# Softmax of two head pairs at once on neighbouring PSUM banks, in a fused attention and MLP kernel

## The chip, the cores and the metric

The kernel runs on one core of one Trainium2 chip. A core has a matrix engine (PE in the profile, with its weight loads shown apart as PEld), a vector engine (DVE), a scalar engine (ACT), a general engine (POOL) and queues that start DMA transfers (SP). Each engine runs its own instructions in the order in which the program holds them, and an instruction that waits for a semaphore holds up all that stand behind it on its engine. The metric is the device time of one execution in microseconds; less is better.

## What is computed

Chunked attention with a short left and right context and eight memory keys, then an MLP with a leaky activation on its output:

```python
B, H, S, D = 4, 8, 768, 64          # batches, heads, tokens, head size
for c in range(S // 32):            # chunks of 32 queries
    keys   = mem_k[8] + k[16 left .. 32 .. 8 right]     # values likewise
    scores = q_c @ keys.T / sqrt(D)
    a      = exp(scores - max(scores));  a /= sum(a) + 1e-9
    out[c] = a @ values
x = out as (3072 tokens, 512)
h = x @ w_in                        # 512 -> 2048
g = max(h, 0) + alpha * min(h, 0)   # alpha per hidden column
y = g @ w_out                       # 2048 -> 512
```

All data are fp32. An fp32 product of the MLP is made of three fp32r products: each operand is split into a high and a low part, and low*high, high*low and high*high are summed in one PSUM bank.

## The kernel before

**Tiling.** The 3072 tokens lie in 8 blocks of 384 (`BT`). A block's attention is cut into four units, one for each pair of heads; unit `u` belongs to block `u // 4`. The MLP of a block is cut into 16 slices `f` of 128 hidden columns.

**Units 0 to 7** (`NWIN`), the attention of blocks 0 and 1, come in the prologue and do the softmax on whole windows (`windows(u)`): scores on PE into a bank of the pool `ps_s` (L271), the maximum on DVE (L439 or L441, then L443), the subtraction (L447), exp on ACT (L451), the sum and its inverse (L455, L458), the scaling on POOL (L468, L472), transposes on PE (`turn`, L480), copies on ACT (L485), the product with the values (L493), and the split of the result into high (ACT, L408) and low (DVE, L412). Score products alternate between two tiles, with tags `s0` and `s1`, each one PSUM bank. `stir` (L257) writes products of a constant tile `busy` that nobody reads: `STIR = (8, 2, 1)` puts 8 of them ahead of the scores of unit 0, 2 ahead of the scores of each other one of the eight units, and 1 ahead of each of the eight turns.

**Units 8 to 31** use other code (L289 to L375), and run between the slices of the blocks ahead of them.

**A slice** `f` of a block has these steps (`hidden`): `up`, 12 products of 128x384 into one bank of `ps_h` (L614, three for each of four parts `k` of x); `below` on ACT, which reads that bank (L623); `bend` on DVE, which reads it too (L626); the high part (ACT or DVE, L632) and low part (DVE, L636) of g; and `down`, 9 products of 128x512 into three banks that collect the block's output (L644). The hidden banks alternate by `place`, the number of the slice in the whole program: tag `h0` for even places, `h1` for odd ones. `ORDER` lets blocks 0 and 1 alternate for their first 9 slices (places 0 to 17); then come the other slices of block 0 and of block 1, and then one block after the other, so that later blocks begin at places 32, 48, 64, 80, 96 and 112.

**Weights** come packed from memory. While block 0 runs, each slice's w_in and w_out are decoded (`decode`, L556 to L583): a gather of half-words (L564, on DVE or on ACT), shifts and joins on DVE, and conversions on ACT and DVE.

**The order of the program.** Each step names the engine, a cost and the keys that it reads and writes (`step` ends in `Plan.add`). `Plan.send` then runs a list scheduler over all steps: it takes an engine's ready step with the longest chain behind it, by the costs and due times, and writes its instructions. So an engine's order is the plan's, and a changed cost or key moves steps far away. The waits, on the other hand, do not come from those keys: they are put in as the instructions are written, by the tiles that they touch. The pools have one buffer for each tag; two tags of a pool are two tiles.

`zero` (L517, L520) clears three buffers of the later units on POOL in the prologue.

Of the kernel before, what the change touches and what calls it, by code (L numbers as in the profile page):

```python
# [9 lines left out]
F32 = mybir.dt.float32  # L10
# [8 lines left out]
P = 128  # L19
# [62 lines left out]

STIR = (8, 2, 1)

DUE_WEIGHTS, DUE_VALUES = 3, 4


NWIN, NSET = 2 * NPAIR, 4

STARTS_WIN = (0, 2 * LEFT, NKT - KW)  # L90
# [66 lines left out]
def body(ctx: ExitStack, tc: tile.TileContext, qvw, kw, first, w_in, w_out, alpha, out):  # L157
# [34 lines left out]

    es = [at.tile([P, NJ * 2, KW + 1], F32, name="e", tag=f"e{i}") for i in range(2)]
    for e in es:
        nc.gpsimd.memset(e[:, :, KW:], 1e-9)
    for ew in ews:
# [61 lines left out]

    def score_products(u):
        blk, pr = divmod(u, NPAIR)  # L260
# [3 lines left out]
        st["s"] = s_ps[:, :2 * NJ * KW].rearrange("p (n k) -> p n k", k=KW)  # L264
        t = early[u % NSET]
        q = t[:, :NQ].rearrange("p (c x) -> p c x", c=NT * NJ)
        keys = t[:, NQ:NQ + NT * NKT].rearrange("p (t k) -> p t k", t=NT)
        for n in range(2 * NJ):
            for i in range(2):
                t, j = n // NJ * 2 + i, n % NJ  # L270
                nc.tensor.matmul(  # L271
                    out=st["s"][i * 2 * CH:(i + 1) * 2 * CH, n],
                    lhsT=q[:, t * NJ + j],
                    rhs=keys[:, t, STARTS_WIN[j]:STARTS_WIN[j] + KW],
                    start=True, stop=True,
                )

    def head_products(u):

        st = state[u]  # L280
        st["s"] = [ps_s.tile([P, 512], F32, name="s_ps", tag=f"s{h2}")[:, :NJ * KW].rearrange("p (n k) -> p n k", n=NJ)
                   for h2 in range(2)]
# [20 lines left out]
    def scores(u):  # L303
# [11 lines left out]
        def exps(i):  # L315
            if i == 0:
                st["e"] = at.tile([P, NJ * 2, KW], F32, name="e", tag=f"e{u % 2}")
                st["den"] = sm.tile([P, NJ * 2, 1], F32, name="den", tag=f"den{u % 3}")
# [7 lines left out]
        for i in range(NJ * 2):  # L326
            step(ACT, 0.54, partial(exps, i), reads=[("s", i % 2), ("mx", u % 3)],
                 writes=[("e", u % 2, i), ("den", u % 3, i)] if i else e_keys(u) + den_keys(u), rest=due(u))

# [89 lines left out]
    def load_first(u):  # L419
# [8 lines left out]
        step(SP, 0.78, partial(load, NQ + NT * NKT, NQ + NT * NKT + NV), writes=[("fv", u % NSET)], rest=due(u))  # L428

    def windows(u):  # L430

        st = state[u]
        sk, tks, ak = ("s", u % 2), [("o", 0), ("o", 1)], ("o", 2) if u % 2 else "a"
        ek = [("ew", u % NPT)]

        def top():
            s = st["s"]
            if u // NPAIR % 2 == 0:
                nc.vector.memset(s[0:2 * CH, 0, 0:LEFT], NEG)  # L439
            else:  # L440
                nc.vector.memset(s[2 * CH:4 * CH, 2 * NJ - 1, KW - NM - RIGHT:KW - NM], NEG)  # L441
            st["mx"] = sm.tile([P, NJ * 2, 1], F32, name="mx", tag=f"mx{u % 3}")
            nc.vector.tensor_reduce(out=st["mx"], in_=s, axis=AX.X, op=ALU.max)  # L443

        def less():
            st["e"] = es[u % 2][:, :, :KW]
            nc.vector.tensor_tensor(out=st["e"], in0=st["s"], in1=st["mx"].broadcast_to([P, NJ * 2, KW]),  # L447
                                    op=ALU.subtract)

        def exps():  # L450
            nc.scalar.activation(out=st["e"], in_=st["e"], func=AF.Exp, scale=SCALE)  # L451

        def total():
            st["den"] = sm.tile([P, NJ * 2, 1], F32, name="den", tag=f"den{u % 3}")
            nc.vector.tensor_reduce(out=st["den"], in_=es[u % 2], axis=AX.X, op=ALU.add)  # L455

        def inverse():
            nc.vector.reciprocal(out=st["den"], in_=st["den"])  # L458

# [39 lines left out]

        step(PE, 1.2, partial(score_products, u), reads=[("qk", u % NSET)], writes=[sk], rest=due(u))  # L500
        step(DVE, 0.66, top, writes=[sk, ("mx", u % 3)])
        step(DVE, 0.55, less, reads=[sk, ("mx", u % 3)], writes=e_keys(u))
        step(ACT, 0.52, exps, writes=e_keys(u))
        step(DVE, 0.56, total, reads=e_keys(u), writes=den_keys(u))
        step(DVE, 0.19, inverse, writes=den_keys(u))
        step(POOL, 0.62, partial(scale, 0), reads=den_keys(u) + e_keys(u), writes=ek)
        step(POOL, 0.5, partial(scale, 1), reads=den_keys(u) + e_keys(u), writes=ek)
        step(PE, 0.90, turn, reads=ek + ["eye"], writes=tks, rest=due(u, 1))
        for t in range(2):
# [37 lines left out]
    def decode_part(k, parts):  # L547
# [53 lines left out]
    def hidden(blk, f, first_f, last_f):  # L601
# [36 lines left out]
        def down(o_ps):  # L638
            if f == first_f:
                banks = [(ps_o, f"o{i}") for i in range(NTT)] if not joint else [(ps_s, "s0"), (ps_s, "s1"), (ps_a, "a")]  # L640
                o_ps.extend(pool.tile([P, DM], F32, name="o_ps", tag=tag) for pool, tag in banks)
            for tt in range(NTT):
# [63 lines left out]
    def unit_begins(u):  # L706
        if u < NWIN:
            windows(u)
        else:
            scores(u)  # L710
# [113 lines left out]
```

## Time and profile before

| | |
|---|---|
| median of three runs | 613.23 us (612.78 to 613.33) |
| the profiled execution, whole | 612.68 us |
| its span, first to last instruction | 610.9 us |
| granted TensorE clock, mean | 1.000 |
| POOL busy | 34.6 us |
| DMA: read and written | 41.95 MB and 6.29 MB |

The span is 1.8 us shorter than the time of the same execution; what lies outside it is start and end. A row of a timeline below reads: start, duration, engine, line and operation, output and inputs with their shapes, the count, and in brackets the idle time ahead of it on its engine and what ended that.

### The profile page before, as it was taken

What the parts mean: (1) busy time and instruction counts of PE and PEld (TensorE: products, weight loads), DVE (VectorE), ACT (ScalarE), POOL (GpSimd) and SP (SyncE); (2) the same over time, 40 slices, a digit from 0 to 9 for tenths busy, and PEclk for the clock granted to TensorE, in tenths of its full rate; (3) what the DMA queues carried; (4) which work ended last, traced back from release to release, by engine and by line L of the source; (5) the groups of instructions that cost most, each with busy time, mean ns of one, the idle gap of its engine ahead of it and who ended that gap; (6) DMA issues with size and microseconds to landing.
All of it is one profiled execution on the core that took longest, in us unless ns stands there. A gap on an engine that the chain in (4) does not pass through costs nothing.

```text
span 610.9 us, 11593 instructions
## 1 busy us (share of the span) xinstructions
PE 605.0 (99%) x4622; PEld 532.9 (87%) x4622; DVE 404.5 (66%) x1012; ACT 215.6 (35%) x596; POOL 34.6 (6%) x61
## 2 busy tenths in 40 slices
PE   8999999999999999999999999999999999999997
PEld 5789999889898888989889889888889888989986
DVE  5888999886777656666666666666666656633332
ACT  3788787634223222322223122322123222121111
POOL 3500000000000000000000000000000000000000
PEclk9999999999999999999999999999999999999999
DMA  8999400114121111201113101221002100010001
GB/s 340 352 408 410 164 0 1 33 32 150 25 96 49 50 50 49 99 3 50 49 50 101 42 9 49 84 67 50 20 30 101 50 18 19 0 54 1 0 1 52
DMA packets 20934, 48.99 MB, mean 80 GB/s; under 512 B 2448, under 2 KB 5520, under 8 KB 20880
## 3 DMA queue, kind: packets, MB, share of 16 engines
q1 hardware_dynamic: 20880, 48.25, 22.3%
q8 instruction: 36, 0.59, 0.4%
q14 instruction: 18, 0.15, 0.1%
HBM read 41.95 MB, written 6.29 MB: 79 GB/s over the span
## 4 chain that ended last, share of the span: by engine, by line
PE 97%; DVE 1%; DMA 1%; issue 0%; ACT 0%; SPq 0%; ACTq 0%
PE h_ps L614 44%; PE o_ps L644 44%; PE a_ps L375 3%; PE s_ps L289 3%; PE s_ps L257 1%; PE s_ps L271 1%; DMA w_t<-w_in 1%; PE a_ps L493 1%; PE o_ps L480 0%; DVE w_t L568 0%; PE o_ps L257 0%; DVE mx L443 0%; DVE e L447 0%; DVE w_t L564 0%; DVE xl L412 0%
## 5 line engine op out<-in xcount | busy, mean ns | idle before, releaser
L614 PE MATMUL h_ps<-xh,w 128*128 128x384 f32 x1024 | 261.6, 336 | 0.0
L644 PE MATMUL o_ps<-w,gh 128*128 128x512 f32 x768 | 240.7, 395 | 0.0
L614 PEld LDWEIGHTS h_ps<-xh,w 128*128 128x128 f32 x1024 | 185.7, 188 | 4.2
L614 PE MATMUL h_ps<-xl,w 128*128 128x384 f32 x512 | 174.6, 341 | 0.1
L644 PEld LDWEIGHTS o_ps<-w,gh 128*128 128x128 f32 x768 | 144.0, 188 | 27.8
L644 PE MATMUL o_ps<-w,gl 128*128 128x512 f32 x384 | 150.1, 391 | 0.0
L623 ACT ACTIVATE g<-h_ps 128x384 f32<-128x384 f32 x128 | 63.4, 496 | 245.2 <-PE h_ps L614 236.0
L626 DVE SCALAR_TENSOR_TENSOR g<-g,rise,h_ps 128x384 f32<-128x384 f32 x128 | 78.3, 612 | 94.4 <-ACT g L623 93.3
L361 DVE STREAM_TRANSPOSE pt<-e 32x192 f32<-32x192 f32 (+1 forms) x336 | 99.3, 300 | 11.1 <-POOL e L340 5.9
L614 PEld LDWEIGHTS h_ps<-xl,w 128*128 128x128 f32 x512 | 96.2, 188 | 6.5 <-DVE xl L412 0.3
L644 PEld LDWEIGHTS o_ps<-w,gl 128*128 128x128 f32 x384 | 72.1, 188 | 12.5
L636 DVE TENSOR_TENSOR gl<-g,gh 128x384 fp32r<-128x384 f32 x128 | 71.1, 557 | 4.6 <-ACT gh L632 1.4
L632 DVE CAST gh<-g 128x384 fp32r<-128x384 f32 x104 | 37.2, 360 | 54.2 <-PE o_ps L644 52.4
L320 ACT ACTIVATE e<-s_ps,mx 128x64 f32<-128x64 f32 x144 | 43.3, 320 | 39.7 <-DVE mx L313 39.7
L340 POOL TENSOR_TENSOR e<-e,den 128x384 f32<-128x384 f32 x24 | 20.1, 839 | 467.1 <-DVE den L337 457.4
L408 ACT CAST xh<-a_ps 128x384 fp32r<-128x384 f32 x32 | 15.4, 480 | 55.4 <-PE a_ps L375 53.6
L320 ACT ACTIVATION_READ_ACCUMULATOR e<-s_ps,mx 128x1 f32 x144 | 30.5, 212 | 0.0
L375 PEld LDWEIGHTS a_ps<-pt,v_t 128*64 128x64 f32 x384 | 16.6, 136 | 8.5 <-issue 8.5
L375 PE MATMUL a_ps<-pt,v_t 128*64 128x96 f32 x384 | 21.1, 252 | 0.0
L583 DVE TENSOR_TENSOR w<-a,w 128x1024 fp32r<-128x1024 f32 (+1 forms) x18 | 20.3, 1135 | 0.0
L572 DVE SCALAR_TENSOR_TENSOR a<-a,w_t 128x1024 int32<-128x1024 int32 (+1 forms) x18 | 19.8, 1102 | 0.2
L556 ACT ACTIVATE a<-w_t 128x1024 f32<-128x1024 f32 (+1 forms) x18 | 18.8, 1048 | 2.9 <-DMA w_t<-w_in 1.6
(52 smaller groups left out, 278.3 us busy)
## 6 DMA issues: line engine op xcount, KB each, us to landing
w_t<-w_in SPq DMA_DIRECT2D x16, 512.0 KB, 10.2
w_t<-w_out SPq DMA_DIRECT2D x16, 512.0 KB, 10.2
qk<-kw SPq DMA_DIRECT2D x24, 272.0 KB, 3.7
v_t<-qvw SPq DMA_DIRECT2D x24, 256.0 KB, 2.8
out<-o_t SPq DMA_DIRECT2D x24, 256.0 KB, 2.1
early<-first SPq DMA_DIRECT2D x8, 656.0 KB, 5.9
qk<-qvw SPq DMA_DIRECT2D x24, 192.0 KB, 3.6
early<-first SPq DMA_DIRECT2D x8, 256.0 KB, 5.9
```

Of the source, the lines that this page charges most:

```text
L320: nc.scalar.activation(out=st["e"][:, i], in_=st["s"][h2][:, n], func=AF.Exp, scale=SCALE, bias=st["mx"][:, n, h2:h2 + 1], accum_out=st["d ...
L340: nc.gpsimd.tensor_tensor(out=st["e"], in0=st["e"], in1=st["den"].broadcast_to([P, NJ * 2, KW]), op=ALU.mult)
L361: nc.vector.transpose(out=pts[u % NPT][quad * CH:(quad + 1) * CH, j, t0:t0 + n1 - n0].rearrange("p t h q -> p (t h) q"), in_=(st["e"], zer ...
L375: nc.tensor.matmul(out=st["a"][h2 * D:(h2 + 1) * D, t * TQ:(t + 1) * TQ], lhsT=st["v"][:, t, h2, :], rhs=pts[u % NPT][:, :, t, h2, :], sta ...
L572: nc.vector.scalar_tensor_tensor(out=d["a"], in0=d["a"], scalar=3, in1=d["t"][:, :, :, 1], op0=ALU.logical_shift_left, op1=ALU.bitwise_or)
L583: nc.vector.tensor_tensor(out=d["w"][:, :, 1], in0=d["a"].bitcast(F32), in1=d["w"][:, :, 0].bitcast(F32), op=ALU.subtract)
L614: nc.tensor.matmul(out=h["ps"][:, :BT], lhsT=ws[f, 0][:, wk, k * P:(k + 1) * P], rhs=xs[first + k][xk], start=(k == 0 and n == 0), stop=(k ...
L623: nc.scalar.activation(out=h["g"], in_=h["ps"][:, :BT], func=AF.Relu, scale=-1.0)
L626: nc.vector.scalar_tensor_tensor(out=h["g"], in0=h["g"], scalar=rise[:, f:f + 1], in1=h["ps"][:, :BT], op0=ALU.mult, op1=ALU.add)
L632: copy(out=h["gh"], in_=h["g"])
L636: nc.vector.tensor_tensor(out=h["gl"], in0=h["g"], in1=h["gh"].bitcast(F32), op=ALU.subtract)
L644: nc.tensor.matmul(out=o_ps[tt], lhsT=h[gk][:, tt * P:(tt + 1) * P], rhs=ws[f, 1][:, wk], start=(f == first_f and i == 0), stop=(f == last ...
```

## The change

- `STIR` becomes `(8, 0, 0)`: 2 unread products go ahead of each of scores 1 to 7, 1 ahead of each of eight turns, 22 in all.
- The two tiles of the pool `ps_s` become one tile `s_banks` of two banks, and the two of `ps_h` one tile `h_banks` of two banks. Everything that used a tile now uses a half: scores and hidden products, and the joint output of block 1's first 9 slices.
- A new function `softmax(us)` does maximum, subtraction, exp, sum and inverse for one or two units with one instruction each. `GROUPS` leaves units 0 and 1 alone and joins 2 with 3, 4 with 5 and 6 with 7. Units 4 and 5 put their scores into `h_banks`, the others into `s_banks`. The exp tiles become two rings of two units.
- `zero` moves from the prologue to the place where block 0's slice 9 is decoded, behind the decoding of slice 8.
- The gather of the half w_out of slice 0 goes from ACT to DVE.
- The plan's costs of a unit's scores and of a turn fall from 1.2 to 0.76 and from 0.90 to 0.68.

```diff
-STIR = (8, 2, 1)
+STIR = (8, 0, 0)
+GROUPS = ((0,), (1,), (2, 3), (4, 5), (6, 7))
...
+    h_banks = ps_h.tile([P, 2, 512], F32, name="h_ps")
+    s_banks = ps_s.tile([P, 2, 512], F32, name="s_ps")
...
-    es = [at.tile([P, NJ * 2, KW + 1], F32, name="e", tag=f"e{i}") for i in range(2)]
+    es = [at.tile([P, 2, NJ * 2, KW + 1], F32, name="e", tag=f"ee{i}") for i in range(2)]
...
-    def score_products(u):
+    def score_products(u, bank):
-        s_ps = ps_s.tile([P, 512], F32, name="s_ps", tag=f"s{u % 2}")
-        stir(s_ps, STIR[0] if u == 0 else STIR[1])
+        stir(bank, STIR[0] if u == 0 else STIR[1])
...
+    def softmax(us):
+        u0, n = us[0], len(us)
+        two, keys = (h_banks, ["h0", "h1"]) if u0 == 4 and n == 2 else (s_banks, [("s", 0), ("s", 1)])
+        here, ring = slice(u0 % 2, u0 % 2 + n), u0 // 2 % 2
+        keys, e = keys[here], es[ring][:, here]
...
+        view = two[:, here, :2 * NJ * KW].rearrange("p b (n k) -> p b n k", k=KW)
+        def top():
...
+            nc.vector.tensor_reduce(out=d["mx"], in_=view, axis=AX.X, op=ALU.max)
+        def less():
+            nc.vector.tensor_tensor(out=e[..., :KW], in0=view, in1=d["mx"].broadcast_to([P, n, NJ * 2, KW]),
+                                    op=ALU.subtract)
...
+        for u, key in zip(us, keys):
+            step(PE, 0.76, partial(score_products, u, two[:, u % 2]), reads=[("qk", u % NSET)], writes=[key], rest=due(u))
+        step(DVE, 0.13 + 0.04 + 0.4 * n + 0.065 * n, top, writes=keys + mk)
+        step(DVE, 0.14 + 0.4 * n, less, reads=keys + mk, writes=ek)
...
-            step(*((ACT, 1.37) if k[1] else (DVE, 0.72)), partial(gather, [nc.scalar.copy if k[1] else nc.vector.tensor_copy]),
-                 writes=r)
+            copy = nc.scalar.copy if k == (1, 1) else nc.vector.tensor_copy
+            step(*((ACT, 1.37) if k == (1, 1) else (DVE, 0.72)), partial(gather, [copy]), writes=r)
...
-                h["ps"] = ps_h.tile([P, 512], F32, name="h_ps", tag=hk)
+                h["ps"] = h_banks[:, place % 2]
...
-            banks = [(ps_o, f"o{i}") for i in range(NTT)] if not joint else [(ps_s, "s0"), (ps_s, "s1"), (ps_a, "a")]
+                if joint:
+                    o_ps.extend([s_banks[:, 0], s_banks[:, 1], ps_a.tile([P, DM], F32, name="o_ps", tag="a")])
...
-    step(POOL, 3.0, zero, writes=["e2"] + [("pt", i, j) for i in range(NPT) for j in range(len(TURNS))] + [("ew", i) for i in range(NPT)])
...
+        if (blk, f) == (0, NJOINT):
+            step(POOL, 3.0, zero, reads=[("w", 1, f - 1, 1)], writes=["e2"] + [("ew", i) for i in range(NPT)]
+                 + [("pt", i, j) for i in range(NPT) for j in range(len(TURNS))])
```

In the prologue, PE's rows begin with the unread products and go on as follows before the change. `early` are the transferred queries and keys of a unit, `ew` the scaled softmax, a name that begins with DMAHW is a transfer's semaphore, and the others are named by their engine; a row with `x11` stands for eleven more alike.

```order
L271 MATMUL s_ps<-early 64x64 [waits DMAHW0_49]
L271 MATMUL s_ps<-early 64x64 x11
L257 LDWEIGHTS busy
L257 MATMUL s_ps<-busy 128x512
L257 LDWEIGHTS busy
L257 MATMUL s_ps<-busy 128x512
L271 MATMUL s_ps<-early 64x64 [waits DMAHW1_49]
L271 MATMUL s_ps<-early 64x64 x11
L257 LDWEIGHTS busy [waits DVE_49]
L257 MATMUL s_ps<-busy 128x512 [waits PE_49]
```

The same place of PE after the change, from the scores of unit 0 to the first turn:

```order
L274 MATMUL s_ps<-early 64x64 [waits DMAHW0_49]
L274 MATMUL s_ps<-early 64x64 x11
L274 MATMUL s_ps<-early 64x64 [waits DMAHW1_49,DVE_49]
L274 MATMUL s_ps<-early 64x64 x11
L274 MATMUL s_ps<-early 64x64 [waits DMAHW2_49,DVE_49]
L274 MATMUL s_ps<-early 64x64 x11
L274 MATMUL s_ps<-early 64x64 [waits DMAHW3_49,DVE_49]
L274 MATMUL s_ps<-early 64x64 x11
L504 MATMUL o_ps<-eye,ew_163 128x128 [waits Pool_49]
```

The unread products are gone, and the scores of unit 1, which waited for their transfer alone, now wait for DVE as well, as do those of units 2 and 3; the values waited for are those that DVE's subtraction of unit 0, maximum of unit 1 and subtraction of unit 1 signal.

Where a block ends and the next begins (places 48 to 50, and likewise at 32, 64, 80, 96 and 112), PE had these rows before, from the fourth part `k` of the slice of place 48 on. A slice has four parts, and a part is the two rows `xl,w` and `xh,w x2`; the split high of the last unit, on ACT, cuts the first one shown in three.

```order
L614 MATMUL h_ps<-xl,w 128x384
L614 MATMUL h_ps<-xh,w 128x384 [waits Activation_49]
L614 MATMUL h_ps<-xh,w 128x384
L614 MATMUL h_ps<-xl,w 128x384
L614 MATMUL h_ps<-xh,w 128x384 x2
L614 MATMUL h_ps<-xl,w 128x384
L614 MATMUL h_ps<-xh,w 128x384 x2
L614 MATMUL h_ps<-xl,w 128x384
L614 MATMUL h_ps<-xh,w 128x384 x2
L614 MATMUL h_ps<-xl,w 128x384
L614 MATMUL h_ps<-xh,w 128x384 x2
L614 MATMUL h_ps<-xl,w 128x384 [waits DVE_49]
```

The first three rows are the fourth part of place 48, the next eight are the slice of place 49 without a wait, and the last is the first product of place 50, which waits for the bend of place 48, in whose bank it writes. After the change, the same stretch of PE, up to the third part of place 49:

```order
L632 MATMUL h_ps<-xl,w 128x384
L632 MATMUL h_ps<-xh,w 128x384 [waits Activation_49]
L632 MATMUL h_ps<-xh,w 128x384
L632 MATMUL h_ps<-xl,w 128x384
L632 MATMUL h_ps<-xh,w 128x384 x2
L632 MATMUL h_ps<-xl,w 128x384 [waits Activation_49]
L632 MATMUL h_ps<-xh,w 128x384 x2
L632 MATMUL h_ps<-xl,w 128x384 [waits DVE_49]
L632 MATMUL h_ps<-xh,w 128x384 x2
L632 MATMUL h_ps<-xl,w 128x384
```

The products stand in the same order, but the slice of place 49 is now cut twice: its second part waits for ACT (the below of place 48) and its third part for DVE (the bend of place 48), while place 50 has no wait of its own left. The steps below and bend of place 48 wait in turn for the products of place 49 that stand ahead of them in the program, though those are in the other bank.

Over the whole program, 98 waits of hidden products on DVE stood in the rows of before, 91 of them for the bend two places back, the last reader of the same bank. After the change there are 114, and 111 of them are for the bend one place back, which reads the other bank of `h_banks`.

More of the change, by code (lines that the diff above doesn't have):

```diff
@@ L257, in stir @@
             nc.tensor.matmul(out=t, lhsT=busy[:, :P], rhs=busy, start=True, stop=True)
-    def score_products(u):
-        blk, pr = divmod(u, NPAIR)
+    def score_products(u, bank):
         st = state[u]
-        s_ps = ps_s.tile([P, 512], F32, name="s_ps", tag=f"s{u % 2}")
-        stir(s_ps, STIR[0] if u == 0 else STIR[1])
-        st["s"] = s_ps[:, :2 * NJ * KW].rearrange("p (n k) -> p n k", k=KW)
+        stir(bank, STIR[0] if u == 0 else STIR[1])
+        s = bank[:, :2 * NJ * KW].rearrange("p (n k) -> p n k", k=KW)
         t = early[u % NSET]
@@ L271, in score_products @@
                 nc.tensor.matmul(
-                    out=st["s"][i * 2 * CH:(i + 1) * 2 * CH, n],
+                    out=s[i * 2 * CH:(i + 1) * 2 * CH, n],
                     lhsT=q[:, t * NJ + j],
@@ L280, in head_products @@
         st = state[u]
-        st["s"] = [ps_s.tile([P, 512], F32, name="s_ps", tag=f"s{h2}")[:, :NJ * KW].rearrange("p (n k) -> p n k", n=NJ)
-                   for h2 in range(2)]
+        st["s"] = [s_banks[:, h2, :NJ * KW].rearrange("p (n k) -> p n k", n=NJ) for h2 in range(2)]
         for n in range(NJ):
@@ L327, in scores @@
             step(ACT, 0.54, partial(exps, i), reads=[("s", i % 2), ("mx", u % 3)],
-                 writes=[("e", u % 2, i), ("den", u % 3, i)] if i else e_keys(u) + den_keys(u), rest=due(u))
+                 writes=[("e", u % 2, i), ("den", u % 3, i)] if i
+                 else e_keys(u) + den_keys(u) + [("ee", u % 2, j) for j in range(2)], rest=due(u))
     def weights(u):
@@ L430, in windows @@
     def windows(u):
         st = state[u]
[L433 to L455, printed above, removed]
@@ L457, in inverse @@
-        def inverse():
-            nc.vector.reciprocal(out=st["den"], in_=st["den"])
+        tks, ak = [("o", 0), ("o", 1)], ("o", 2) if u % 2 else "a"
+        ek, dk, eu = [("ew", u % NPT)], [("dw", u // 2 % 2, u % 2)], [("ee", u // 2 % 2, u % 2)]
         def scale(part):
@@ L498, in values @@
                     )
[L500 to L508, printed above, removed]
+        step(POOL, 0.62, partial(scale, 0), reads=dk + eu, writes=ek)
+        step(POOL, 0.5, partial(scale, 1), reads=dk + eu, writes=ek)
+        step(PE, 0.68, turn, reads=ek + ["eye"], writes=tks, rest=due(u, 1))
         for t in range(2):
@@ L639, in down @@
             if f == first_f:
-                banks = [(ps_o, f"o{i}") for i in range(NTT)] if not joint else [(ps_s, "s0"), (ps_s, "s1"), (ps_a, "a")]
-                o_ps.extend(pool.tile([P, DM], F32, name="o_ps", tag=tag) for pool, tag in banks)
+                if joint:
+                    o_ps.extend([s_banks[:, 0], s_banks[:, 1], ps_a.tile([P, DM], F32, name="o_ps", tag="a")])
+                else:
+                    o_ps.extend(ps_o.tile([P, DM], F32, name="o_ps", tag=f"o{i}") for i in range(NTT))
             for tt in range(NTT):
@@ L707, in unit_begins @@
         if u < NWIN:
+            for us in GROUPS:
+                if us[0] == u:
+                    softmax(us)
             windows(u)
```

25 lines of the change are left out of this document (23 added, 2 removed).

## The prediction

> **What bounds the kernel now.** I read the page first, for the busy shares, the chain that ended last and the groups.
>
> ```profile
> PE 605.0 (99%) x4622; PEld 532.9 (87%) x4622; DVE 404.5 (66%) x1012; ACT 215.6 (35%) x596; POOL 34.6 (6%) x61
> PE 97%; DVE 1%; DMA 1%; issue 0%; ACT 0%; SPq 0%; ACTq 0%
> L623 ACT ACTIVATE g<-h_ps 128x384 f32<-128x384 f32 x128 | 63.4, 496 | 245.2 <-PE h_ps L614 236.0
> L626 DVE SCALAR_TENSOR_TENSOR g<-g,rise,h_ps 128x384 f32<-128x384 f32 x128 | 78.3, 612 | 94.4 <-ACT g L623 93.3
> ```
>
> PE is busy 605.0 of 610.9 us and is 97% of the chain. Next, the busy times by stretch: the prologue, block 0 with the decoding, the change to block 2, the later blocks, the end. The columns are the stretch, its length, then PE, PEld, DVE, ACT and POOL busy, the granted clock, the DMA share and GB/s.
>
> ```profile
> 0.00:35.00 35.00, 32.77 (x416) 22.98 (x416) 25.49 (x62) 19.97 (x41) 14.44 (x37) 1.00 0.94 353
> 35.00:140.00 105.00, 105.00 (x673) 94.12 (x670) 92.42 (x159) 75.50 (x125) 1.89 (x2) 1.00 0.37 140
> 140.00:200.00 60.00, 60.00 (x484) 53.46 (x482) 43.60 (x127) 18.55 (x72) 3.32 (x4) 1.00 0.22 73
> 200.00:600.90 400.90, 400.90 (x3029) 357.46 (x3029) 241.44 (x663) 99.37 (x356) 14.94 (x18) 1.00 0.13 42
> ```
>
> From 35 us to 600.9 us PE has no gap at all. Two things follow. Only less PE work, or fewer gaps in the first 35 us (35.00 less 32.77, 2.2 us of them), can make the kernel faster. And any wait newly put into PE's row after 35 us is paid in full, since nothing there is idle that it could hide in. In the stretch 35 to 140, DVE is busy 92.42 of 105.00, so results of DVE come late there.
>
> **Part 1: the unread products.** Last I read PE's timeline in the prologue.
>
> ```profile
> 1.45 3.60 PE L257 MATMUL s_ps<-busy 128*128 128x512 bf16 x8 [1.45 <-DVE warm L199]
> 4.98 1.55 PE L271 MATMUL s_ps<-early 128*64 128x64 f32 x24
> 6.46 0.60 PE L257 MATMUL s_ps<-busy 128*128 128x512 bf16 x2
> 7.00 0.92 PE L271 MATMUL s_ps<-early 128*64 128x64 f32 x24
> 7.92 0.61 PE L257 MATMUL s_ps<-busy 128*128 128x512 bf16 x2
> ...
> 17.00 0.39 PE L257 MATMUL o_ps<-busy 128*128 128x512 bf16 x1
> 17.23 0.82 PE L480 MATMUL o_ps<-eye,ew 128*128 128x128 f32 x6
> ```
>
> Two of them take 6.46 to 7.00, 0.54 us; one ahead of a turn takes 17.00 to 17.23, about 0.22. Gone are 7 x 0.54 + 8 x 0.22 = 5.5 us of PE. That is the largest gain the change can have. It is not all on the path: what the scores wait for is also the transfers, and the turns wait for the softmax.
>
> **Part 2: the prologue's waits.** Before, the scores of unit 1 follow those of unit 0 without a gap. After, unit 1's scores wait for DVE's subtraction of unit 0, though it reads the other bank, those of unit 2 for the maximum of unit 1, and those of unit 3 for its subtraction. The DVE rows of unit 0 give the price.
>
> ```profile
> 6.61 0.07 DVE L439 MEMSET s_ps<- 64x16 f32 x1 [5.21 <-PE s_ps L271]
> 6.72 0.56 DVE L443 TENSOR_REDUCE mx<-s_ps 128x6 f32<-128x384 f32 x1
> 7.31 0.56 DVE L447 TENSOR_TENSOR e<-s_ps,mx 128x384 f32<-128x384 f32 x1
> ```
>
> The scores end 6.53, the subtraction 7.87; with 0.05 for the signal, scores 1 begin at 7.92 instead of 6.46 + 0 (the unread products gone): 1.4 us. In the same way I price units 2 and 3: scores 0.92 (0.85 to the next issue), memory set and maximum 0.7, subtraction 0.56, one gap each of some 0.7 to 0.8: 1.5. A pair's softmax has no row; two sizes of the maximum bound it:
>
> ```profile
> L310 DVE TENSOR_REDUCE mx<-s_ps 128x3 f32<-128x192 f32 x48 | 17.2, 359 | 1.6
> L443 DVE TENSOR_REDUCE mx<-s_ps 128x6 f32<-128x384 f32 x8 | 4.5, 557 | 0.3
> L468 POOL TENSOR_TENSOR ew<-e,den 128x256 f32<-128x256 f32 x8 | 4.9, 618 | 16.1 <-DVE s_ps L439 7.1 <-DVE den L458 3.2 <-ACT qk L485 1.8
> ```
>
> 192 elements more cost 0.20 us, so 384 more make 0.557 into 0.95, between 0.557 and 1.11. DVE gains some 0.15 on each of the three long instructions of a pair, little of it on PE's path. But DVE's row now holds the maximum of units 6 and 7 ahead of the sum of 4 and 5, and so unit 4's turn waits for unit 7's scores, the last to arrive: maximum 0.95, sum 0.95, subtraction 0.95, inverse 0.2, POOL's first scaling 0.62 and signals of 0.3 make 4.0 us, beside which PE has two turns and two values, 2 x (0.75 + 0.81) = 3.1 (a turn's issue, and values up to the next row). That is 0.9 idle, and some 0.6 more while POOL scales the second part: 1.5. Small waits of the other turns for that second scaling and of unit 7 for its transfer add 1.7. Idle time of 1.4 + 1.5 + 1.5 + 1.7 = 6.1 stands against 5.5 saved: **+0.6 us**, with ends -1.4 (the waits for the softmax alone, none of the coupled scores: 3.2 of idle, and 0.9 of gaps that were there) and +5 (all of it, and the products behind the gaps slower).
>
> Of the clock: the first eight unread products took 0.43 us each after start, later ones 0.27, and unit 0's scores 1.55 against 0.92 later; in this execution full speed came at some 6.5 us and the granted clock stays at 1.00 in every stretch. [...]
>
> **Part 3: other moves.** The gather goes from 1.39 us on ACT to 0.77 on DVE, and `zero` (0.56 + 2 x 0.74 of POOL) leaves the prologue.
>
> ```profile
> L564 ACT COPY w_t<-w_t 128x512 int16<-128x512 int16 x14 | 19.5, 1391 | 0.1
> L564 DVE COPY w_t<-w_t 128x512 int16<-128x512 int16 x14 | 10.7, 767 | 1.9 <-ACT a L556 1.9
> L520 POOL MEMSET pt<- 128x768 f32 x2 | 1.5, 738 | 2.3 <-PE o_ps L480 2.3
> ```
>
> Neither is on PE. Behind slice 8's decoding POOL has 1.89 us busy in the 105 us stretch, so `zero` has room, and unit 8, its first user, comes later. I put both at 0, with ends -0.6 (the gather's own length off the wait for slice 0's weights) and +0.9 (its length ahead of a softmax on DVE).
>
> **Part 4: the block boundaries.** The six places where a block ends and the next begins run hidden products of two and a half slices in a row, 30 of them, with no `down` between. Rows of one, PE, ACT and DVE by start:
>
> ```profile
> 248.91 0.33 PE L614 MATMUL h_ps<-xl,w 128*128 128x384 f32 x1
> 249.08 0.51 PE L614 MATMUL h_ps<-xh,w 128*128 128x384 f32 x2
> 249.10 0.49 ACT L623 ACTIVATE g<-h_ps 128x384 f32<-128x384 f32 x1 [1.17 <-PE h_ps L614]
> 249.43 0.33 PE L614 MATMUL h_ps<-xl,w 128*128 128x384 f32 x1
> 249.63 0.61 DVE L626 SCALAR_TENSOR_TENSOR g<-g,rise,h_ps 128x384 f32<-128x384 f32 x1 [0.43 <-ACT g L623]
> 249.95 0.33 PE L614 MATMUL h_ps<-xl,w 128*128 128x384 f32 x1
> ```
>
> Place 49's first part begins at 248.91 while ACT and DVE still read place 48's bank (to 250.24). In the changed program below(48) first waits for that first part, which ends at 249.59: it runs 249.62 to 250.11, and the second part, which now waits for it, begins at 250.17 instead of 249.43, 0.74 us late. That part ends at 250.85; bend runs 250.88 to 251.49, and the third part begins at 251.55, where it would have stood at 250.69: 0.86 more. A boundary costs 1.6 us, and with longer signals up to 1.8. Six times 1.7 is **+10.2 us**, with ends 6 x 1.40 = 8.4 (place 49 as a whole waiting for a bend that ends at 250.24: 250.30 less 248.91) and 6 x 2.8 = 16.8 (this wait also at place 50).
>
> **Part 5: while weights are decoded, 35 to 192 us.** With a `down` of 9 products between two slices the bend is done in time when DVE is free: seven slices past place 49 it ends at 278.64, and the next slice begins at 279.38.
>
> ```profile
> 278.02 0.62 DVE L626 SCALAR_TENSOR_TENSOR g<-g,rise,h_ps 128x384 f32<-128x384 f32 x1 [1.20 <-ACT g L623]
> ...
> 279.38 0.33 PE L614 MATMUL h_ps<-xl,w 128*128 128x384 f32 x1
> ```
>
> So the steady loop of later blocks costs 0, with 0.7 us to spare. In the stretch with decoding the bend is late or there are two slices in a row:
>
> ```profile
> 111.45 0.33 PE L614 MATMUL h_ps<-xl,w 128*128 128x384 f32 x1
> ...
> 112.34 0.59 DVE L626 SCALAR_TENSOR_TENSOR g<-g,rise,h_ps 128x384 f32<-128x384 f32 x1
> ```
>
> Here the slice that starts at 111.45 would have to wait for a bend that ends at 112.93: 1.5 us. I took this difference, bend's end plus 0.06 less the next slice's start, for every slice of the stretch outside the boundaries and the first four slices: eleven are above zero by 0.22 to 3.14 us, 13.8 together. That is an upper end, since PE, once late, gives DVE time and the next bend comes earlier against it. Laid out with the changed rows, their waits and the durations of this trace, where each wait moves what follows on PE but not the decoding on DVE, some ten gaps of 0.4 to 2.0 us stay: **+9.5 us**, with ends +4 and +14. One more of 0.9 comes at the last unit, near 565 us.
>
> **The sum.** 0.6 + 0 + 10.2 + 9.5 + 0.9 = 21.2 us on the profiled execution of 612.68: 633.9. The median of the runs is 0.55 higher than that execution; I forecast **634.2 us** (a ratio of 1.034).
>
> **The rivals.**
>
> *A, the forecast: joint tiles couple their banks.* For it: the waits stand in the program's rows, 111 of 114 for the bend one place back, and PE has no slack (105.00 of 105.00). Against: none of the prices was seen as a wait. 621 to 643 us. Chance 0.87.
>
> *B, the other side: the coupling costs little, the products' removal is worth its face.* The mechanism: two banks worked on by different engines do not hold each other up, since the waits are already satisfied when PE gets there, and the prologue loses its unread products. From PE's rows the gain is at most 5.5; the transfer of unit 7, and then the pair 6 and 7 through the softmax, bound it to some 1.4 us: 612.7 - 1.4 = 611.3, up to 607.7 if all 5.5 come through. It decides from the point where bend(p-1) ends ahead of slice p in all places, which the row at 249.63 contradicts by 1.40 us. Chance 0.05. [...]
>
> *C, mild coupling.* Only the boundaries at their low end and a little of the decoding stretch are paid: 612.7 + 8.4 + 2 = 623 us, 621 to 625. This is inside A's range at its low end; I count 0.06 of A for it.
>
> *D, the prologue loses speed too.* Gaps there slow the products that follow to what the first eight showed (0.43 against 0.27): 8 us of products would take 8 x (0.43/0.27 - 1) = 4.7 us more, 639 us. Chance 0.06.
>
> *E, no difference.* The prologue's gain of some 1.4 and a few waits cancel: 612 to 614. Chance 0.02.
>
> **How the numbers follow.** Faster by over 0.2% (1.2 us, about what a measurement of this kernel can tell from no change) comes from B alone, 0.05; within 0.2% 0.02; slower 0.93. The range leaves out B and E and the outer parts of A and D: from 612.7 - 1.4 + 8.4 + 4 = 623.7, rounded to 623, to 612.7 + 0.6 + 16.8 + 9.5 + 0.9 + 1.5 = 642, the last 1.5 for a part of D.
>
> **What would show it.** In the changed profile: PE busy falls by 5.5 us, and the page's waits of PE, which show nothing after 35 us now, list hidden products waiting for bend and for below, near 20 us together. The busy times by stretch show PE below the stretch in 35 to 200, and in 200 to 600 by 8 to 10 us, all at the boundaries: one gap of 0.7 to 0.9 us before the second part and one before the third part of places 49, 65, 81, 97 and 113. The scores of unit 1 wait for DVE's subtraction. I am wrong if the boundaries are dense, or if the granted clock falls, or if gaps of the prologue exceed 11 us.

## The result, and the profile after

The changed kernel takes 637.14 us (median of 6 runs, 635.57 to 637.68) against 613.24 us, a ratio of 1.0387 with a 95% interval of 1.0374 to 1.0401. The forecast was 634.2 us. Its profiled execution takes 636.8 us with a span of 635.0, so 24.1 us more than the profiled one of before.

The page of the changed kernel, lines that answer to those of before (L641 is below, L644 is bend):

```profile
PE 608.7 (96%) x4600; PEld 532.2 (84%) x4600; DVE 403.5 (64%) x1001; ACT 214.0 (34%) x592; POOL 34.0 (5%) x61
PE 93%; DVE 4%; ACT 1%; issue 1%; POOL 0%; DVEq 0%; ACTq 0%; POOLq 0%
L644 DVE SCALAR_TENSOR_TENSOR g<-g,rise,h_ps 128x384 f32<-128x384 f32 x128 | 78.3, 613 | 132.3 <-ACT g L641 108.8
L641 ACT ACTIVATE g<-h_ps 128x384 f32<-128x384 f32 x128 | 62.7, 492 | 274.6 <-PE h_ps L632 260.5
```

The instructions cost what they cost before (613 and 492 ns, 612 and 496 there), and DVE has less to do. But 5% of the chain is now DVE and ACT, and PE, idle for 5.9 us before (610.9 less 605.0), is idle for 26.3. The busy times by stretch of the changed kernel, in the columns used above:

```profile
0.00:35.00 35.00, 29.06 (x379) 22.60 (x381) 23.27 (x48) 17.95 (x37) 14.07 (x37) 0.90 0.87 313
35.00:140.00 105.00, 101.33 (x603) 89.36 (x601) 85.88 (x135) 74.16 (x120) 0.83 (x1) 1.00 0.38 149
140.00:200.00 60.00, 54.34 (x502) 46.29 (x501) 42.21 (x127) 16.54 (x61) 3.32 (x4) 1.00 0.22 70
200.00:600.90 400.90, 393.46 (x2976) 347.12 (x2975) 241.63 (x674) 100.62 (x367) 15.77 (x19) 1.00 0.14 43
```

Each stretch that was dense has gaps: 3.7, 5.7 and 7.4 us. PE's waits in the whole changed kernel, by what was waited for (total, times, longest, in us); before, this list had the unread products' two rows alone, 1.5 and 0.6 us, both in the prologue:

```profile
PE h_ps L632 <- DVE g L644: 8.6, 11, 0.9
PE h_ps L632 <- ACT g L641: 3.8, 7, 0.6
PE o_ps L664 <- DVE gl L654: 2.1, 2, 1.7
PE s_ps L274 <- DVE e L455: 2.0, 2, 1.4
...
PE o_ps L504 <- POOL ew L492: 1.3, 2, 1.1
...
PE h_ps L632 <- DVE s_ps L301: 1.1, 1, 1.1
PE s_ps L274 <- DVE mx L452: 0.8, 1, 0.8
```

Hidden products wait for bend and below, and the scores of units 1 to 3 for the softmax in the other bank (2.0 and 0.8 us in the list). The timeline at places 48 to 50 shows one such pair of waits, in PE, ACT and DVE rows by start:

```profile
262.52 0.33 PE L632 MATMUL h_ps<-xl,w 128*128 128x384 f32 x1
262.69 0.51 PE L632 MATMUL h_ps<-xh,w 128*128 128x384 f32 x2
263.24 0.49 ACT L641 ACTIVATE g<-h_ps 128x384 f32<-128x384 f32 x1 [1.69 <-PE h_ps L632]
...
263.79 0.44 PE L632 MATMUL h_ps<-xl,w 128*128 128x384 f32 x1 [0.58 <-ACT g L641]
264.06 0.51 PE L632 MATMUL h_ps<-xh,w 128*128 128x384 f32 x2
264.68 0.61 DVE L644 SCALAR_TENSOR_TENSOR g<-g,rise,h_ps 128x384 f32<-128x384 f32 x1 [1.86 <-PE h_ps L632]
265.35 0.44 PE L632 MATMUL h_ps<-xl,w 128*128 128x384 f32 x1 [0.77 <-DVE g L644]
```

PE and the two engines that read its banks now take turns: a part of place 49 on PE, below of place 48 on ACT, a part on PE, bend on DVE, and PE again. Before, all of this lay side by side.

Where the 24.1 us arise shows when the same work of PE is done in both traces. For this all products but the unread ones are counted, each kind with its usual distance to the next one, and the moments are compared at which equal sums stand done:

| at, in the trace of before | what lies up to there | the changed kernel is later by |
|---|---|---|
| 40 us | the prologue | 1.1 |
| 100 us | decoding | 3.9 |
| 140 us | decoding | 7.1 |
| 160 us | end of the decoding stretch | 9.7 |
| 200 us | the first boundary, and a wait for the low part of g behind it | 13.6 |
| 300 us | the second | 15.5 |
| 400 us | the third and fourth | 19.4 |
| 500 us | the fifth | 21.3 |
| 600 us | the sixth, and one wait more behind it | 24.1 |

The delay grows by 1.90 to 1.93 at each boundary from the second to the fifth, and does not change between them. Two waits beside those of the boundaries stand out, behind the first and behind the sixth:

```profile
193.07 0.50 PE L664 MATMUL o_ps<-w,gl 128*128 128x512 f32 x1 [1.70 <-DVE gl L654]
...
572.62 0.44 PE L632 MATMUL h_ps<-xl,w 128*128 128x384 f32 x1 [0.66 <-DVE g L644]
```

### The profile page after: what moved, and what is told of

Read it like the earlier page. It is cut to its first block, busy times and chain, and to the rows that moved or that the text cites. A ratio compares the mean times of both kernels' runs of the same rounds, so it can differ in the third digit from the quotient of the medians.

```text
span 635.0 us, 11508 instructions
## 1 busy us (share of the span) xinstructions
PE 608.7 (96%) x4600; PEld 532.2 (84%) x4600; DVE 403.5 (64%) x1001; ACT 214.0 (34%) x592; POOL 34.0 (5%) x61
## 4 chain that ended last, share of the span: by engine, by line
PE 93%; DVE 4%; ACT 1%; issue 1%; POOL 0%; DVEq 0%; ACTq 0%; POOLq 0%
PE h_ps L632 44%; PE o_ps L664 38%; PE a_ps L378 3%; PE s_ps L291 2%; DVE g L644 2%; PE s_ps L664 2%; ACT g L641 1%; PE o_ps L504 1%; PE s_ps L274 1%; PE a_ps L517 1%; PE s_ps L262 1%; DVE mx L452 0%; PE h_ps L274 0%; DVE e L455 0%; DVE gl L654 0%
## 5 line engine op out<-in xcount | busy, mean ns | idle before, releaser
L664 PE MATMUL o_ps<-w,gh 128*128 128x512 f32 x732 | 229.4, 395 | 0.0
L632 PE MATMUL h_ps<-xl,w 128*128 128x384 f32 x512 | 176.7, 345 | 13.6 <-DVE g L644 8.6
L644 DVE SCALAR_TENSOR_TENSOR g<-g,rise,h_ps 128x384 f32<-128x384 f32 x128 | 78.3, 613 | 132.3 <-ACT g L641 108.8
L664 PEld LDWEIGHTS o_ps<-w,gh 128*128 128x128 f32 x732 | 137.3, 188 | 26.6
L641 ACT ACTIVATE g<-h_ps 128x384 f32<-128x384 f32 x128 | 62.7, 492 | 274.6 <-PE h_ps L632 260.5
L664 PE MATMUL o_ps<-w,gl 128*128 128x512 f32 x366 | 143.3, 392 | 2.1 <-DVE gl L654 2.1
L632 PEld LDWEIGHTS h_ps<-xl,w 128*128 128x128 f32 x512 | 96.1, 188 | 27.0 <-DVE g L644 15.5
L664 PEld LDWEIGHTS o_ps<-w,gl 128*128 128x128 f32 x366 | 68.8, 188 | 14.8 <-DVE gl L654 2.8
## 6 DMA issues: line engine op xcount, KB each, us to landing
w_t<-w_in SPq DMA_DIRECT2D x16, 512.0 KB, 10.2
w_t<-w_out SPq DMA_DIRECT2D x16, 512.0 KB, 10.2
```

The source lines that it names most:

```text
L632: nc.tensor.matmul(out=h["ps"][:, :BT], lhsT=ws[f, 0][:, wk, k * P:(k + 1) * P], rhs=xs[first + k][xk], start=(k == 0 and n == 0), stop=(k ...
L641: nc.scalar.activation(out=h["g"], in_=h["ps"][:, :BT], func=AF.Relu, scale=-1.0)
L644: nc.vector.scalar_tensor_tensor(out=h["g"], in0=h["g"], scalar=rise[:, f:f + 1], in1=h["ps"][:, :BT], op0=ALU.mult, op1=ALU.add)
L664: nc.tensor.matmul(out=o_ps[tt], lhsT=h[gk][:, tt * P:(tt + 1) * P], rhs=ws[f, 1][:, wk], start=(f == first_f and i == 0), stop=(f == last ...
```

## The experiments

Times are medians beside runs of the kernel before on the same chip; ratios are to these, with 95% intervals. The first group asks which of the tiles costs how much.

**Two lines of the change, in the kernel before: the hidden banks as one tile.**

```diff
+    h_banks = ps_h.tile([P, 2, 512], F32, name="h_ps")
...
-                h["ps"] = ps_h.tile([P, 512], F32, name="h_ps", tag=hk)
+                h["ps"] = h_banks[:, place % 2]
```

> The kernel before with one line changed: the two hidden banks are one tile of two banks. Theory: the wait alone costs what it costs in the changed kernel, 10 us at the boundaries and about 10 in the first 200 us, 630 to 636 us. Rival (the coupling costs only where the changed order puts slices back to back): 622 to 625 us.

Measured: 637.42 us, ratio 1.039 (1.0375 to 1.0406). That is 24.0 us more than before, as much as the whole change, and above the range of the theory. The order of PE is that of before, and so are the instructions and their sizes; the waits alone differ, so the price does not hang on the changed order. PE's waits from 200 us on in this kernel:

```profile
PE h_ps L615 <- DVE g L627: 4.5, 6, 0.8
PE h_ps L615 <- ACT g L624: 2.9, 5, 0.6
```

In the changed kernel the same stretch has 4.5 us in 6 waits and 2.9 us in 5 as well: the five later boundaries and one slice behind the last.

**The changed kernel with a tile for each bank.** The order of PE is the changed one; a pair's maximum and subtraction are written as one instruction for each bank.

```diff
-    h_banks = ps_h.tile([P, 2, 512], F32, name="h_ps")
-    s_banks = ps_s.tile([P, 2, 512], F32, name="s_ps")
+    h_banks = [ps_h.tile([P, 512], F32, name="h_ps", tag=f"h{i}") for i in range(2)]
+    s_banks = [ps_s.tile([P, 512], F32, name="s_ps", tag=f"s{i}") for i in range(2)]
...
-            nc.vector.tensor_reduce(out=d["mx"], in_=view, axis=AX.X, op=ALU.max)
+            for i, view in enumerate(views):
+                nc.vector.tensor_reduce(out=d["mx"][:, i * w:(i + 1) * w], in_=view, axis=AX.X, op=ALU.max)
```

> The changed kernel in the changed order, but each PSUM bank is a tile of its own again; a pair's maximum and subtraction are written as one instruction for each bank (12 instead of 6), exp, sum and inverse stay joined. Theory (the joint tiles couple their banks): the 24 us go, 612 to 614 us, no hidden product waits for a bend one place back. Rival (the new order, the unread products' removal and the moved clearing cost it): 630 us or more, as nothing of these is undone.

Measured: 612.57 us, ratio 0.9989 (0.9979 to 0.9998). The 24 us are gone with the rest of the change in place, but for the pairs' maximum and subtraction. PE's waits in the whole of this kernel are these four, all in the prologue; the rows of hidden products are gone:

```profile
PE s_ps L274 <- DMA early<-first: 1.9, 3, 0.7
PE s_ps L274 <- DVE den L475: 1.8, 1, 1.8
PE s_ps L262 <- DVE warm L204: 1.5, 1, 1.5
PE s_ps L274 <- DVE mx L459: 0.8, 1, 0.8
```

**The changed kernel with the hidden banks apart, the score banks still one tile** (the same edit for `h_banks` alone).

> The changed kernel with only the hidden banks as two tiles (units 4 and 5 then have two instructions for maximum and subtraction); the score banks stay one tile. Theory: the boundaries and the stretch of decoding are dense again, only the prologue keeps its waits for DVE: 613 to 617 us. Rival (the coupled score banks make most of it, by late starts in the prologue): 625 us or more.

Measured: 613.64 us, ratio 1.0005 (0.9996 to 1.0015). So the joint hidden tile costs 23.5 us of the changed kernel's time. The joint score tile costs about 1 at most: the ranges of this run and the one above, 612.32 to 614.65 and 611.77 to 613.89, do not tell the two apart.

**The kernel before with the score banks as one tile**, the unread products kept (likewise for the scores of the later units and the joint output):

```diff
+    s_banks = ps_s.tile([P, 2, 512], F32, name="s_ps")
...
-        s_ps = ps_s.tile([P, 512], F32, name="s_ps", tag=f"s{u % 2}")
+        s_ps = s_banks[:, u % 2]
```

> The kernel before with the two score banks as one tile (unread products kept). Theory: scores 1 to 3 wait for DVE's work on the bank beside it, and the prologue gets some 4 to 6 us longer, 616 to 619 us; after 40 us nothing. Rival (late transfers hide those waits): 613 to 614 us.

Measured: 619.79 us, ratio 1.0102 (1.0083 to 1.0121), slightly more than expected. PE's timeline of this kernel in the prologue:

```profile
10.16 1.00 PE L258 MATMUL s_ps<-busy 128*128 128x512 bf16 x2 [1.39 <-DVE mx L444]
11.09 1.55 PE L272 MATMUL s_ps<-early 128*64 128x64 f32 x24
13.30 1.01 PE L258 MATMUL s_ps<-busy 128*128 128x512 bf16 x2 [0.66 <-DVE e L448]
14.24 1.55 PE L272 MATMUL s_ps<-early 128*64 128x64 f32 x24
```

PE waits for DVE five times here, 5.1 us in all, where the kernel before waits twice, 0.6 us, and behind each wait come unread products, now on the path; the two rows of them above took 1.00 and 1.01 us, 0.60 before, with a granted clock of 0.78 from 8 to 12 us and 0.50 from 12 to 16. In the changed kernel there are none, and the same tile costs some 5 us less there. That the products behind the waits make this difference is likely but not shown: the order of the prologue differs too, and the changed kernel with the score banks joint and the unread products was not run.

The second group asks what the other parts are worth once the banks are apart.

**The kernel before without the 22 unread products.**

```diff
-STIR = (8, 2, 1)
+STIR = (8, 0, 0)
```

> The kernel before without the 22 unread products (STIR (8, 0, 0)), all else the same, tiles apart as before. Theory: of the 5.5 us of PE work only what does not turn into waits for transfers and softmax comes through, about 1 us: 612.0 to 612.8. Rival 1 (all of it is on the path): 608. Rival 2 (the products keep the clock up, and without them the prologue runs at half speed in part): 614 to 617, with a granted clock below 0.9 somewhere in 8 to 28 us.

Measured: 612.91 us, ratio 0.9994 (0.9985 to 1.0003): not told from no change. The first 35 us of this kernel, against 32.77 us of PE in that of before:

```profile
0.00:35.00 35.00, 26.84 (x392) 20.81 (x394) 25.95 (x62) 19.81 (x41) 13.94 (x37) 1.00 0.95 365
```

PE lost 5.9 us of work and got 5.9 us of idle time for it. The products lay in time in which PE would have waited for transfers and softmax: by this kernel's list of waits 2.3 us for transfers, and 3.5 us for maximum, subtraction and sum on DVE and the copies behind the turns on ACT. The granted clock is 1.00 there without them in the profiled run; one of the eleven runs has a mean of 0.997.

**Every unit alone, a tile for each bank.**

```diff
-GROUPS = ((0,), (1,), (2, 3), (4, 5), (6, 7))
+GROUPS = ((0,), (1,), (2,), (3,), (4,), (5,), (6,), (7,))
```

> The changed kernel with a tile for each bank and every unit alone (no pairs): tells what the joining of two units' softmax is worth. Theory: pairs save DVE little and make a unit wait for its neighbour, so this is faster than the one with pairs and banks apart (612.57): 610.5 to 612. Rival (a pair's fewer DVE instructions pay): 613 to 615.

Measured: 611.08 us (610.88 to 611.28), ratio 0.9965 (0.9952 to 0.9977). This is faster than the kernel before and than the one with pairs, whose runs begin at 611.77. The version with pairs takes 1.5 us more; how much of that is the joining itself is not shown, since the plan's order of the prologue changes with the groups, and the last experiment shows that order alone can move this kernel as far. Its first 35 us:

```profile
0.00:35.00 35.00, 30.65 (x402) 23.11 (x403) 26.39 (x65) 20.07 (x43) 14.51 (x37) 1.00 0.92 341
```

Without the unread products PE is busy for 30.65 us there, 3.8 us more than in the run above.

**The unread products put back, with pairs and banks apart** (`STIR = (8, 2, 1)`).

> The changed kernel with a tile for each bank and the unread products put back (STIR (8, 2, 1)). If the half clock seen at 16 to 24 us in the one without them (granted 0.76 and 0.81) comes from their removal and costs what they cost, this is equal, 612.5 to 613.5, with the clock at 1.00 throughout. If they are pure load on the path, 615 to 618.

Measured: 612.62 us, ratio 0.9990 (0.9981 to 0.9999), equal to 612.57 without them. The clock is at 1.00 throughout the prologue, and all eleven runs have a mean of 0.999 or more. Without them four of the ten runs have 0.997, the profiled one among them, and their median is 613.1 us against 612.3 of the other six. The next version shows the like: five of its eleven runs have 0.997, with a median of 614.3 against 613.3. So a stretch at a lowered clock seems to cost these two versions 0.8 to 1.0 us when it comes, though the runs are few.

**Another use of the banks for pairs**: units 0, 1, 4 and 5 alone on hidden banks apart, pairs 2 with 3 and 6 with 7 on the joint score banks.

```diff
-GROUPS = ((0,), (1,), (2, 3), (4, 5), (6, 7))
+GROUPS = ((0,), (1,), (2, 3), (4,), (5,), (6, 7))
...
-        two, keys = (h_banks, ["h0", "h1"]) if u0 == 4 and n == 2 else (s_banks, [("s", 0), ("s", 1)])
+        two, keys = (h_banks, ["h0", "h1"]) if n == 1 else (s_banks, [("s", 0), ("s", 1)])
```

> Hidden banks apart; units 0, 1, 4 and 5 alone on them, pairs 2 with 3 and 6 with 7 on the joint score banks, no unread products. No scores wait for DVE's work on the neighbour of their bank ahead of unit 6. Theory: the prologue loses the 2.9 us of such waits that the run with the hidden banks apart had (613.64), but a part goes into later waits: 611.5 to 613. Rival (transfers set the prologue): as that one, 613.6.

Measured: 613.71 us, ratio 1.0008 (0.9999 to 1.0016): the rival. The 2.9 us of scores' waits for DVE went, and other waits of PE came in their place: those for transfers grew from 1.4 to 3.0 us (three, the longest 1.7), and one product with the values waits 2.1 us for the low part of a split (DVE, L415).

The third group undoes one part each in the version with every unit alone (611.08).

**The clearing back in the prologue** (the step of `zero` at its old place).

> The version with every unit alone and a tile for each bank (611.08), with the clearing of the three buffers back in the prologue. Theory: POOL has room there, no change, 610.8 to 611.4. Rival (its 2 us of POOL stand ahead of a scaling, or slow a DVE copy beside it): 611.8 to 613.

Measured: 611.27 us, ratio 0.9967 (0.9954 to 0.9979): no difference.

**The gather back on ACT.**

```diff
-            copy = nc.scalar.copy if k == (1, 1) else nc.vector.tensor_copy
+            copy = nc.scalar.copy if k[1] else nc.vector.tensor_copy
```

> The same version (611.08) with the gather of the half w_out of slice 0 back on ACT. Theory: 0.6 us longer in the gather itself, but not on the path of PE: 610.8 to 611.6. Rival (slice 0's weights are what PE waits for at the end of the prologue): 611.7 to 613.

Measured: 611.35 us, ratio 0.9972 (0.9960 to 0.9983): 0.3 us more, too little to be told from none.

**The unread products put back.**

> The same version (611.08) with the 22 unread products put back. Theory: without coupled waits and pairs PE is dense enough that a part of the 5.5 us is on the path: 612 to 614. Rival (as with pairs, where putting them back changed nothing, 612.62 against 612.57): 610.8 to 611.5.

Measured: 612.52 us, ratio 0.9992 (0.9983 to 1.0001): 1.4 us more, in the same order of PE. Here, where PE is denser, a quarter of the 5.5 us is on the path.

**The plan's old costs for scores and turn.**

```diff
-            step(PE, 0.76, partial(score_products, u, bank(u % 2)), reads=[("qk", u % NSET)], writes=[key], rest=due(u))
+            step(PE, 1.2, partial(score_products, u, bank(u % 2)), reads=[("qk", u % NSET)], writes=[key], rest=due(u))
...
-        step(PE, 0.68, turn, reads=ek + ["eye"], writes=tks, rest=due(u, 1))
+        step(PE, 0.90, turn, reads=ek + ["eye"], writes=tks, rest=due(u, 1))
```

> The same version (611.08) with the plan's old costs for a unit's scores and turn (1.2 and 0.90), which only changes the order that the plan chooses. Theory: the order in the prologue is what separates this version from the kernel before without unread products (612.91), so it goes back to 612.3 to 613.2. Rival (the order matters little): 610.8 to 611.6.

Measured: 612.55 us, ratio 0.9984 (0.9975 to 0.9993): 1.5 us come from the order alone. With the old costs the plan's order leaves PE's first hidden products waiting 1.3 us for slice 0's decoded weights on DVE, with the new ones 0.5. That accounts for the 0.7 us between the two profiled executions (611.96 and 611.26); the rest of the 1.5 between the medians is in no trace that was kept. The two ranges of the last two runs (611.57 to 612.71 and 612.17 to 613.26) do not reach those of 611.08, 610.88 to 611.28.

## Why the prediction held, point by point

- **The coupling of the banks** (rival A, 0.87) is the cause, shown from both sides: it makes 24.0 us alone in the kernel before, and without it the changed kernel is at 612.57. Rival B, no coupling, priced at 611.3, is what the changed kernel is with a tile for each bank: 612.57, which is 0.9 us under the 613.43 beside it, of that rival's 1.4. Rivals C (the boundaries and a little of the decoding, at most 625) and E (no difference) fall: the decoding stretch is paid, 8.6 us of it.
- **Part 4, the boundaries:** 1.6 us was worked out and 1.7 taken; 1.9 was measured. The waits are those forecast: ACT's row begins 0.04 us behind the first part, and the second part comes 0.06 behind ACT's end. What was left out: a hidden product behind a gap takes 0.44 us instead of 0.33 (263.79 and 265.35), and the next starts 0.27 behind it instead of 0.17. Bend, too, begins 0.11 us behind the second part (264.57 to 264.68), where 0.03 was taken. Twice 0.1 and 0.08 make most of the difference.
- **A wait without a term:** the first boundary adds 3.9 us, of which 2.0 are not the boundary's two gaps. The row at 193.07 shows it: `down` waits 1.70 us for the low part. The below of place 33 now begins only when the products of place 34 are done (191.41), its bend follows, and the low part of place 32 stands behind that bend on DVE. The prediction looked at waits of hidden products alone and put nothing for those of `down`.
- **Part 5, the decoding:** 9.5 us forecast, 8.6 measured (from 40 to 160 us, 9.7 less 1.1). So this term was somewhat too high. The list of waits alone would make it too small, as at a boundary, where 0.58 + 0.77 = 1.35 us of idle time stand for 1.9 lost: a gap is counted from the end that the profile shows for the product ahead of it, 263.20 at places 48 to 50, where the next product, at the usual distance of 0.17 us, would have begun at 263.03.
- **The last unit:** 0.9 forecast, and measured: from 500 to 600 us 2.84 are added, of which 1.93 is the boundary. It is the wait at 572.62, which answers to 548.5 in the trace of before and not to some 565: the size was right, the place was not.
- **Part 2, the prologue:** +0.6 forecast, +1.1 at 40 us. The gap ahead of unit 1's scores was priced at 1.4 and is 1.39, units 2 and 3 at 1.5 together and are 0.80 and 0.65, unit 4's turn at 1.5 and waits 1.07 and 0.29. The 1.7 for small waits of the other turns and of unit 7 came as 0.2. By the same counting as in the table, PE's gaps grew by 3.7 us, its products took 2.9 us longer, above all where the granted clock was 0.73 (8 to 12 us) and 0.50 (12 to 16), and 5.6 us of unread products were gone. The forecast's sum had no term for slow products; only rival D had. That the prologue came out near is in part luck. A row of the changed kernel's prologue for each:

```profile
7.92 0.92 PE L274 MATMUL s_ps<-early 128*64 128x64 f32 x24 [1.39 <-DVE e L455]
9.64 1.45 PE L274 MATMUL s_ps<-early 128*64 128x64 f32 x24 [0.80 <-DVE mx L452]
11.74 1.55 PE L274 MATMUL s_ps<-early 128*64 128x64 f32 x24 [0.65 <-DVE e L455]
...
25.02 0.44 PE L504 MATMUL o_ps<-eye,ew 128*128 128x128 f32 x2 [1.07 <-POOL ew L492]
25.75 0.66 PE L504 MATMUL o_ps<-eye,ew 128*128 128x128 f32 x4 [0.29 <-POOL ew L496]
```

- **A pair's instructions** were put at 0.95 us for the maximum from two sizes; the groups of the changed kernel show 958 ns for the maximum of 12 rows:

```profile
L452 DVE TENSOR_REDUCE mx<-s_ps 128x12 f32<-128x768 f32 x2 | 1.9, 958 | 0.1
L455 DVE TENSOR_TENSOR e<-s_ps,mx 128x768 f32<-128x768 f32 x2 | 1.9, 952 | 0.0
```

- **Rival D, the clock**, came in part: the granted clock of the changed kernel falls to a half behind those gaps in the profiled run, as the stretches of its prologue show (the last three columns are the clock, the DMA share and GB/s):

```profile
8.00:12.00 4.00, 2.54 (x52) 2.22 (x54) 1.75 (x5) 0.71 (x2) 0.03 (x1) 0.73 1.01 394
12.00:16.00 4.00, 4.00 (x54) 3.55 (x52) 2.71 (x6) 1.20 (x3) 2.21 (x6) 0.50 0.99 339
```

It did not add the 4.7 us. Two of the six runs of the changed kernel have a mean clock of 0.994 (636.6 and 636.8 us), one has 0.999 (635.6), three have 1.000 (637.5, 637.5 and 637.7), so the runs with the lowered clock are not the longer ones. The prediction named a falling clock as a sign of being wrong; the sign came, and the forecast held beside it. Here it fell behind gaps of 1.39 and 0.80 us; in the kernel before, where the longest gap of PE in the prologue, once it has begun, is 0.4 us by the list of waits, it is 1.00 in every stretch.
- **Wrong in the list of what the profile would show:** PE's busy time was to fall by 5.5 us and rose by 3.7. Slow products count as busy: scores took 1.45 to 1.55 us instead of 0.92 where the granted clock was 0.73 and 0.50. The begin of a gap counts too where the end shown for the product ahead covers it (263.03 to 263.20, as above). The delay of equal work, not the sum of busy time, shows such a change. The waits of hidden products for bend and below were to be near 20 us; 8.6 and 3.8 are listed, for the same reason. The gaps at the boundaries stand where forecast, listed with 0.58 and 0.77 us, and the busy time from 200 us on is 7.4 us below the stretch, where 8 to 10 were forecast.
- **Part 3** (gather and clearing, 0 us): 0.3 and 0.2 us in the version with every unit alone, less than a measurement of this kernel can tell.
- **Part 1:** that the products' removal is not worth 5.5 us was right, and is now measured: 0.5 us in the kernel before, 0.05 with pairs and banks apart (neither can be told from none), 1.4 with every unit alone and the plan's new costs.

The forecast of 634.2 is 2.9 us short of 637.14. (633.9 and the 0.55 named beside it make 634.4, not 634.2.) By the profiled executions the terms are 1.1 for the prologue, 8.6 for the decoding, 11.5 for six boundaries of 1.9, 0.9 for the last and 2.0 for the wait of `down`, 24.1 together, instead of 0.6, 9.5, 10.2, 0.9 and nothing, 21.2. The mechanism was right. What was missed most is the wait of `down` at the first boundary, then the price of a boundary; that the decoding was put too high hid 0.9 us of this.

## What to carry to other kernels

Two buffers that shall overlap must be two tiles, or whatever the program's waits are kept by: a joint view of neighbouring banks for one wide instruction in a prologue put a wait for the neighbouring bank into nearly every slice of the main loop here, and the joint hidden tile alone cost 24.0 us in the kernel before. Before a change of buffers, list for each wait on the bounding engine which instruction it stands for before and after; a wait that moves from two steps back to one is paid where no other work lies between, here at six boundaries (11.5 us) and during the decoding (8.6 us). A filler on the bounding engine that lies in idle time gives nothing back when it is removed, until something else can take its place: the 22 unread products here gave 0.5 us in the kernel before, not told from none, and 1.4 us with every unit alone.

## What was not expected of the hardware

In the profiled run of the changed kernel the granted clock fell: 0.73 on the mean from 8 to 12 us, 0.50 from 12 to 16. Up to there no gap of PE behind its first product was longer than 1.39 us, and from 8 to 12 us PE was idle for 1.46 us. In the kernel before without its unread products, PE idle for 8.2 us of the first 35, it stayed at 1.00 in the profiled run. In the kernel before with the score banks as one tile it fell as well, 0.78 and 0.50 in the same stretches, with the unread products in place.

The gaps alone do not decide it. The changed kernel with the hidden banks apart has gaps of like length ahead of its scores (by its list of waits two for the subtraction, 2.1 us with the longest 1.4, and one of 0.8 for the maximum), and its profiled run shows 1.00 in every stretch up to 40 us. And runs of one and the same kernel differ: two of six runs of the changed kernel have a mean of 0.994, the other four 0.999 or 1.000. What makes the clock fall in one run and not in another was not settled.
